# Where the row maxima of an attention kernel get their PSUM tiles: single tiles throughout, or from step 140 on pairs of maxima that share three score tiles with the scores

## The chip, the cores and the metric

The kernel runs on one core of one Trainium2 chip. The metric is the device time of one execution in microseconds (us). The kernel before takes 1129.84 us, the median of three runs from 1128.42 to 1130.21. "Step 140" and the like are numbers of attention steps, counted from 0, and are explained below.

## The reference

In short form: one block of a transformer on 2048 tokens of width 448, in float32: a layer norm with a modulation from the vector `c`, full attention with 16 heads of 28 columns, its output projection, a gate and a residual, then a second modulated layer norm and a channel MLP (448 to 1792 to 448, GELU) with its own gate and residual.

```python
mod = (_silu(c) @ w_mod).reshape(c.shape[0], 6, 1, -1)
sa, ca, ga, sb, cb, gb = (mod[:, i] for i in range(6))
h = _layernorm(x) * (1 + ca) + sa
q, k, v = (h @ wqkv) split into 16 heads of 28
p = softmax(q @ k.T * 28 ** -0.5)
x = x + ga * ((p @ v) @ wo)
h = _layernorm(x) * (1 + cb) + sb
x = x + gb * (gelu(_layernorm(h) @ w1 + b1) @ w2 + b2)
```

## The kernel before

The program has three stretches: a first one that makes queries, keys and values (up to about 169 us of the profile), the attention loop (169 to 833 us) and the MLP. The change is in the attention loop.

**Units and steps.** The 16 heads make four groups `g` of four heads, and the 2048 queries four blocks `qt` of 512. One pair (g, qt) is a unit, 16 units in all, and each unit walks through the 2048 keys in 16 steps (`kt`) of 128 keys. So there are 256 steps; step = 16 u + kt.

**What a step does.** For each half of the four heads (two heads) TensorE computes scores, 128 keys on the partitions by 512 queries for two heads, into one score tile of two PSUM banks (`s0` or `s1`, 128x2x512 floats). A score is the sum of three matmuls per head, since every operand is split into a high and a low float32r part; that makes 6 matmuls per half and 12 per step (line 1162). A matmul of one head uses 28 or 29 of the 32 rows of one of TensorE's four row groups: the first half of the heads lives in row groups 0 and 1, the second in 2 and 3. In the text, S1 is the half that is written first in a step and S2 the other. ScalarE takes the exponential of a whole score tile (line 1167), once per half. Then TensorE multiplies the exponentials of the step before with the values (line 1132, "output products", into tile `o`), with all 128 rows.

**Row maxima.** The softmax subtracts each query's maximum before the exponential. It goes into the score matmul as a 29th row of the queries, so it has to be known before the unit starts. A maximum is computed for 128 queries of one head over 512 keys: one matmul of the high parts alone (line 466, in one row group) into a single PSUM bank, and one reduction on VectorE from there (line 471). A unit needs 64 of these; they stand in a queue `mxq` that is sorted by unit. When a unit's 64 are done, `max_fin` reduces over the key blocks (line 502), and two steps later `put` transposes the result (line 509) and sends it into the unit's query tile with four DMAs. `finish_max` computes what is left of the next unit's maxima, at key step 10 of each unit.

**PSUM.** Eight banks: `o` has one, `s0` and `s1` two each, `m1` one, and `m2` two tiles of one bank each. In the attention loop single maxima take turns in `m1`, `m2`, `m2`. When no maximum is left, `third_tile` gives the two banks of `m2` to a third score tile `s2`.

**What sets the order.** Everything is written out by hand (`manual_schedule`): the engines take their instructions in the order of the Python code, and the framework adds semaphores where a tile is still in use. It tracks a tile as a whole, not its halves. `n_maxima` gives 4 maxima to even steps and 3 to odd ones. They are written between the score matmuls of the step: one or two behind the first terms of S1, in the row groups of S2, and the rest behind the last term of S2.

**Projection.** In the last group, and already for the last block of the group before, the output of a finished unit is multiplied with `wo` in key steps 8 to 11 of the next unit (`t_wo`, one product of 128 tokens per step, "projection steps": 200 to 203, 216 to 219, 232 to 235 and 248 to 251). It takes 9 or 12 matmuls of 448 columns (line 386) into a tile of `m1` or `m2`, and ScalarE copies it out (line 926). Its input goes a long way first: the unit's output is copied to `osb` (line 1101), its denominators go to DRAM and back, are inverted on VectorE (line 886) and broadcast by DMA; GpSimd multiplies (line 895, `t_split`), VectorE rounds (line 905, the high part `hi`, in `t_split2`) and GpSimd subtracts (line 906, the low part). The plan in `unit_end_tasks` puts `t_split2` five steps behind the first task of a unit's end. In steps 228 to 235 the first layer norm of the MLP stretch also starts (lines 190, 191, 207, on VectorE).

## Time and profile before

| what | value |
|---|---|
| median of three runs | 1129.84 us |
| profiled execution | 1130.08 us |
| its span, first to last instruction | 1128.0 us |
| TensorE clock granted | 1.000 |
| attention steps 140 to 235 | 514.85 to 778.13 us |
| maxima in steps 140 to 233 | 323 |

In the profile's rows PE is TensorE's matmul, PEld its weight load, DVE is VectorE, ACT is ScalarE, POOL is GpSimd and SP is SyncE, which issues DMAs. A row reads: start, duration, engine, line, operation, output tile <- input tiles (buffer numbers are left out, so `s` is any score tile and `m` any tile of a single maximum), partitions x elements, count; in brackets the idle time ahead of it and what ended it. In rows of groups the two numbers behind the bar are busy time in us and mean duration in ns.

### The profile page before, as it was taken

The numbers are of one execution on the slowest core, as the hardware profiler recorded it, in microseconds if no ns is written. First come the engines' busy times: TensorE is split into PE (matmuls) and PEld (weight loads), VectorE is DVE, ScalarE is ACT, GpSimd is POOL, SyncE is SP. The second block draws the span as 40 slices with busy tenths as digits, with TensorE's granted clock in tenths as the row PEclk, the third lists the DMA queues.
The fourth block names the chain that finished last, engine by engine and source line by source line (L and its number), as shares of the span: only waits on it lengthen the run. The fifth ranks groups of instructions, "written<-read, shape, count | busy, mean of one in ns | idle before, by whom it ended". The sixth has DMA issues, their size and how long they took to land.

```text
span 1128.0 us, 20665 instructions
## 1 busy us (share of the span) xinstructions
PE 1116.4 (99%) x8319; PEld 670.1 (59%) x8319; DVE 843.7 (75%) x1485; ACT 672.0 (60%) x823; POOL 209.6 (19%) x211
## 2 busy tenths in 40 slices
PE   8999999999999999999999999999999999999998
PEld 6756674444444444444444454545468888888887
DVE  6968788999999999999999978595448853444322
ACT  4555657888887888788788867576752321111110
POOL 1533332110000000000000020217114504123000
PEclk9999999999999999999999999999999999999999
DMA  9562263121121211311111312020422100000000
GB/s 303 202 200 88 91 200 114 48 84 41 58 95 57 58 40 57 91 53 58 53 44 58 112 41 83 4 85 1 137 73 78 35 33 1 1 33 1 33 1 33
DMA packets 49341, 81.19 MB, mean 72 GB/s; under 512 B 12311, under 2 KB 18702, under 8 KB 49234
## 3 DMA queue, kind: packets, MB, share of 16 engines
q1 hardware_dynamic: 48762, 79.14, 22.1%
q8 instruction: 65, 1.06, 0.4%
q10 hardware_dynamic: 148, 0.46, 0.1%
q0 software_dynamic: 336, 0.28, 0.1%
q14 instruction: 30, 0.25, 0.1%
HBM read 55.04 MB, written 26.48 MB: 72 GB/s over the span
## 4 chain that ended last, share of the span: by engine, by line
PE 94%; DVE 3%; ACT 1%; DMA 1%; issue 1%; POOL 0%; SPq 0%; DVEq 0%; ACTq 0%; POOLq 0%
PE s L1162 26%; PE o L1132 22%; PE m L386 16%; PE pa L386 8%; PE m L466 6%; PE s L1232 3%; PE s L1233 3%; PE s L1231 3%; DVE mxp L471 2%; PE t L1232 1%; PE t L1233 1%; PE t L1231 1%; DMA slot_c<-in_w_mod_dram 1%; PE ma L466 1%; PE o L267 1%
## 5 line engine op out<-in xcount | busy, mean ns | idle before, releaser
L471 DVE TENSOR_REDUCE mxp<-m 128x1 f32<-128x512 f32 x884 | 568.8, 686 | 75.3 <-PE m L466 41.1
L1162 PE MATMUL s<-slot_b,slot_a 28*128 28x512 f32 (+1 forms) x3072 | 376.3, 420 | 0.0
L1162 PEld LDWEIGHTS s<-slot_b,slot_a 28*128 28x128 f32 (+1 forms) x3072 | 213.0, 184 | 247.4 <-ACT slot_c L1167 124.1
L466 PE MATMUL m<-kh,qh 28*128 28x512 f32 x863 | 287.6, 472 | 1.2 <-DVE mxp L471 0.9
L1167 ACT ACTIVATE slot_c<-s 128x1024 f32<-128x1024 f32 x170 | 174.3, 1025 | 75.9 <-PE s L1162 75.6
L1132 PE MATMUL o<-slot_c,v 128*32 128x512 f32 x680 | 178.8, 605 | 0.0
L1208 ACT ACTIVATE full<-m,b_col 128x512 f32<-128x512 f32 x56 | 38.6, 689 | 192.0 <-PE m L386 175.5
L1132 PE MATMUL o<-slot_c1h,v 128*32 128x512 f32 x512 | 134.7, 605 | 0.0
L1132 PE MATMUL o<-slot_c0h,v 128*32 128x512 f32 x512 | 134.7, 605 | 0.0
L1167 ACT ACTIVATE slot_c0h<-s 128x1024 f32<-128x1024 f32 x128 | 130.4, 1019 | 2.4 <-PE m L386 2.4
L1167 ACT ACTIVATE slot_c1h<-s 128x1024 f32<-128x1024 f32 x128 | 130.4, 1019 | 0.0
L1211 DVE CAST hi<-full 128x512 fp32r<-128x512 f32 x56 | 25.5, 455 | 134.6 <-ACT full L1208 134.6
L466 PEld LDWEIGHTS m<-kh,qh 28*128 28x128 f32 x863 | 114.3, 182 | 8.6 <-DVE mxp L471 5.1
L1167 ACT ACTIVATE slot_d<-s 128x1024 f32<-128x1024 f32 x86 | 88.1, 1025 | 39.3 <-PE s L1162 39.1
L895 POOL TENSOR_TENSOR osb<-osb,osb 128x512 f32<-128x512 f32 x16 | 20.9, 1307 | 441.1 <-DMA osb<-drec 356.8
L1132 PE MATMUL o<-slot_d,v 128*32 128x512 f32 x344 | 90.5, 605 | 0.4 <-ACT osb L1101 0.4
L386 PE MATMUL m<-y,slot_a 128*128 128x512 f32 x160 | 60.7, 395 | 0.0
L1132 PEld LDWEIGHTS o<-slot_c,v 128*32 128x32 f32 x680 | 24.5, 108 | 52.4 <-issue 49.5
L1212 DVE TENSOR_TENSOR lo<-full,hi 128x512 fp32r<-128x512 f32 x56 | 44.2, 788 | 5.9 <-DVE hi L1211 0.9
L471 DVE TENSOR_REDUCE mxp<-ma 128x1 f32<-128x512 f32 x54 | 35.6, 683 | 7.1 <-PE m L466 4.8
L386 PE MATMUL m<-y,slot_v 128*128 128x512 f32 x112 | 39.2, 396 | 0.0
L386 PE MATMUL m<-y,slot_b 128*128 128x512 f32 x112 | 39.0, 398 | 0.0
(316 smaller groups left out, 1626.7 us busy)
## 6 DMA issues: line engine op xcount, KB each, us to landing
slot_b<-d SPq DMA_DIRECT2D x32, 256.0 KB
slot_a<-d SPq DMA_DIRECT2D x32, 256.0 KB
d<-lo SPq DMA_DIRECT2D x28, 256.0 KB
d<-hi SPq DMA_DIRECT2D x16, 256.0 KB
osb<-drec SPq DMA_DIRECT2D x15, 256.0 KB
out_dram<-xn SPq DMA_DIRECT2D x16, 224.0 KB
raw<-in_B_w_dram SPq DMA_DIRECT2D x14, 224.0 KB
qh<-d SPq DMA_DIRECT2D x12, 256.0 KB
```

The source lines that it names most:

```text
L386: pe.matmul(p, a, b, start=(i == 0), stop=(i == len(terms) - 1))
L466: pe.matmul(m, qh_sb[(g, qt)][js, i * 128 : (i + 1) * 128], k[js, :], start=True, stop=True)
L471: dve.tensor_reduce(out=mxp[(g, qt)][:, i, j, cch : cch + 1], in_=m, op=ALU.max, axis=AX.X)
L1132: pe.matmul(o[32 * j : 32 * j + 32, :], v_sb[kt // 4][:, kt % 4, 4 * g + j, :], p[j // 2][:, j % 2, :], start=(kt == 0), stop=(kt == NKT - 1),
L1162: pe.matmul(s2[:, jj, :], ks[rows_, kp, kc], qs[rows_, qp, :], start=(term == 0), stop=(term == 2))
L1167: act.activation(pt[hf], s2, AF.Exp, scale=SCALE)
L1208: act.activation(gf, p, AF.Gelu_apprx_tanh, bias=b1_col[:, i : i + 1])
L1211: dve.tensor_copy(ghi, gf)
L1212: dve.tensor_tensor(out=glo, in0=gf, in1=f(ghi), op=ALU.subtract)
L1231: pe.matmul(pp, ghi[:, ts], w_hi, start=(m == 0), stop=False)
L1232: pe.matmul(pp, ghi[:, ts], w_lo, start=False, stop=False)
L1233: pe.matmul(pp, glo[:, ts], w_hi, start=False, stop=(m == NFT - 1))
```

## The change

Nothing is changed in the computation. Ahead of step 140 step 0 computes two maxima fewer, and the choice of the next maximum is a little different. From step 140 on (`RING`):

- The tiles of `m2` are given up at step 140, and `s2` exists from there on. S1 always goes into `s0`. `s1` and `s2` take turns: in one step the one holds the scores of S2 and the other a pair of maxima, in the next step the other way round. Which half of the heads is S1 alternates from step to step.
- A step computes three maxima: one single in `m1`, behind the first term of S1, and one pair, two neighbouring heads of the same queries and keys, ahead of the last term of S2 (`emit_pair`). A pair is two matmuls into the two halves of one score tile and one reduction of 128x2x512 on VectorE (line 614). A fourth maximum comes only where `extra` finds that the steps left won't do; it does so once, at step 193.
- In a projection step `t_wo` writes a second pair into `s0` and a single into the second half of the score tile that this step's S2 has used, and then the projection itself into the first half of that same tile. That makes six maxima.
- `finish_max` comes at key step 12 instead of 10, and `ready_max` passes only maxima whose query and key tiles have been loaded three steps ago.

In the built program steps 140 to 235 hold 325 maxima, of them 104 pairs; the last is in step 235 (before: in step 233). In steps 200 to 203, 216 to 219 and 232 to 234 there are six per step, and `finish_max` finds four left ahead of step 220.

The core of the diff:

```diff
+LAST_MAX = NKT - 4
+RING = 140
...
+    def emit_single(half, ps):
+        near = ready_max()
...
+        max_one(g, qt, cch, i, j, ps)
+        count(g, qt, [cch])
+
+    def emit_pair(half, t):
+        near = ready_max()
+        for a, m in enumerate(near):
+            n = m[:4] + (m[4] + 1,)
+            if m[4] == 2 * half and n in near:
+                mxq.remove(m)
+                mxq.remove(n)
+                g, qt, cch, i, j = m
+                for jj in range(2):
+                    max_mm(g, qt, i, j + jj, kh_sb[(g, cch)], lambda: t[:, jj])
+                dve.tensor_reduce(out=mxp[(g, qt)][:, i, j : j + 2, cch], in_=t, op=ALU.max, axis=AX.X)
+                count(g, qt, [cch, cch])
+                return
+        for jj in range(2):
+            emit_single(half, lambda: t[:, jj])
...
         def t_wo(t):
             def go():
-                p = ps_mx()
+                if three:
+                    p = ps_mx()
+                else:
+                    emit_pair(0, ps_two("s0"))
+                    two = ps_two(now[0])
+                    emit_single(1, lambda: two[:, 1])
+                    p = two[:, 0]
...
-            if kt == NKT - 6 and u + 1 < NU:
+            clock[0] = step
+            if kt == LAST_MAX and u + 1 < NU:
                 finish_max(*divmod(u + 1, NB))
...
+            now[0] = turns[step % 2]
+            first = step % 2 if step >= RING else 0
+            if step == RING:
                 third_tile(True)
+            ring = step >= RING
+            more = ring and not three and extra(step)
+            late_one, after = after, more
+            n_max = 0 if ring else 4 - step % 2
...
-            for hf in range(2):
-                s2 = ps_s2()
+            for n, hf in enumerate((first, 1 - first)):
+                s2 = ps_s2() if three else ps_two((now[0] if n else "s0") if ring else ("s0", "s1")[n])
                 for term, (kp, qp) in enumerate(((0, 0), (1, 0), (0, 1))):
+                    if ring and n == 1 and term == 2 and mxq:
+                        emit_pair(first, ps_two(turns[1 - step % 2]))
                     for jj in range(2):
                         rows_ = slice(64 * hf + 32 * jj, 64 * hf + 32 * jj + DH + (term == 0))
                         pe.matmul(s2[:, jj, :], ks[rows_, kp, kc], qs[rows_, qp, :], start=(term == 0), stop=(term == 2))
...
+                    if ring and (n, term) == ((1, 0) if late_one else (0, 0)) and not three:
+                        emit_single(1 - first, ps_mx)
```

Three places of TensorE's order follow, of the program before and of the changed one. Lines 1162, 466, 1132 and 386 (scores, maxima, output products, projection) are lines 1228, 470, 1188 and 390 in the changed kernel. `s0`, `s1`, `s2`, `m1`, `m2` and `o` are the PSUM tiles, with numbers of their uses behind them; `slot_a` and `slot_b` hold keys and queries for the scores, `kh` and `qh` those for the maxima, `slot_c`, `slot_d` the exponentials. In brackets are the engines that a row waits for ("Activation" is ScalarE).

First, TensorE in one plain step of three maxima, step 143 of the program before:

```order
L1162 MATMUL s1_1695_7078<-slot_b0_1442_6028,slot_a3_1567_6552 128x512 [waits Activation_49]
L1162 MATMUL s1_1695_7078<-slot_b0_1442_6028,slot_a3_1567_6552 128x512
L466 MATMUL m1_1696_7081<-kh0_1107_4625,qh3_1226_5113 128x512 [waits DVE_49]
L1162 MATMUL s1_1695_7078<-slot_b0_1442_6028,slot_a3_1567_6552 128x512 x4
L1162 MATMUL s0_1697_7089<-slot_b0_1442_6028,slot_a3_1567_6552 128x512 [waits Activation_49]
L1162 MATMUL s0_1697_7089<-slot_b0_1442_6028,slot_a3_1567_6552 128x512 x5
L466 MATMUL m2_1698_7096<-kh0_1107_4625,qh3_1226_5113 128x512 [waits DVE_49]
L466 MATMUL m2_1699_7099<-kh0_1107_4625,qh3_1226_5113 128x512 [waits DVE_49]
L1132 MATMUL o_1577_6591<-slot_c0_1685_7042,v3_231 32x512 x2
L1132 MATMUL o_1577_6591<-slot_c0h_1686_7043,v3_231 32x512 x2
```

and step 151 of the changed program:

```order
L1228 MATMUL s0_1744_7317<-slot_b1_1574_6581,slot_a1_1499_6268 128x512 [waits Activation_49]
L1228 MATMUL s0_1744_7317<-slot_b1_1574_6581,slot_a1_1499_6268 128x512
L470 MATMUL m1_1745_7320<-kh2_1203_5028,qh3_1250_5224 128x512 [waits DVE_49]
L1228 MATMUL s0_1744_7317<-slot_b1_1574_6581,slot_a1_1499_6268 128x512 x4
L1228 MATMUL s2_1746_7328<-slot_b1_1574_6581,slot_a1_1499_6268 128x512 [waits DVE_49]
L1228 MATMUL s2_1746_7328<-slot_b1_1574_6581,slot_a1_1499_6268 128x512 x3
L470 MATMUL s1_1747_7333<-kh1_1231_5149,qh3_1250_5224 128x512 [waits Activation_49]
L470 MATMUL s1_1747_7333<-kh1_1231_5149,qh3_1250_5224 128x512
L1228 MATMUL s2_1746_7328<-slot_b1_1574_6581,slot_a1_1499_6268 128x512 x2
L1188 MATMUL o_1699_7122<-slot_d0_1736_7286,v1_229 32x512 x2
L1188 MATMUL o_1699_7122<-slot_c0h_1737_7287,v1_229 32x512 x2
```

The two maxima behind S2 have become a pair in a score tile ahead of the last term of S2; S2 waits for VectorE instead of ScalarE, and the pair for ScalarE.

Second, TensorE in projection step 217 from S2 (before) on; the first two products of the projection end the piece:

```order
L1162 MATMUL s0_2327_9735<-slot_b1_2110_8812,slot_a2_2068_8639 128x512 [waits Activation_49]
L1162 MATMUL s0_2327_9735<-slot_b1_2110_8812,slot_a2_2068_8639 128x512 x5
L466 MATMUL m2_2328_9742<-kh0_1717_7166,qh3_1832_7642 128x512 [waits Activation_49]
L1132 MATMUL o_2248_9411<-slot_d0_2313_9672,v2_230 32x512 x2
L1132 MATMUL o_2248_9411<-slot_c0h_2314_9673,v2_230 32x512 x2
L386 MATMUL m1_2329_9750<-slot_e0_489_2037,slot_a2h_2258_9448 128x448 [waits DVE_49]
L386 MATMUL m1_2329_9750<-slot_e1_490_2038,slot_a2h_2258_9448 128x448
```

and in the changed program from the last term of S2 on:

```order
L1228 MATMUL s2_2214_9491<-slot_b1_2028_8623,slot_a2_1994_8469 128x512 x2
L1188 MATMUL o_2149_9199<-slot_d0_2201_9427,v2_230 32x512 x2
L1188 MATMUL o_2149_9199<-slot_c0h_2202_9428,v2_230 32x512 x2
L470 MATMUL s0_2216_9507<-kh3_1833_7720,qh2_1689_7068 128x512 [waits Activation_49]
L470 MATMUL s0_2216_9507<-kh3_1833_7720,qh2_1689_7068 128x512
L470 MATMUL s2_2217_9511<-kh0_1727_7243,qh3_1835_7725 128x512 [waits Activation_49]
L390 MATMUL s2_2217_9511<-slot_e0_489_2037,slot_a2h_2158_9234 128x448 [waits DVE_49]
L390 MATMUL s2_2217_9511<-slot_e1_490_2038,slot_a2h_2158_9234 128x448
```

A pair in `s0` and a single in `s2` stand between the output products and the projection, and the projection's first product, into that same `s2`, waits for VectorE. The count that this wait asks for is reached by the reduction of the single just ahead of it.

Third, TensorE between steps 219 and 220: the last product of the projection, and then, before:

```order
L386 MATMUL m2_2347_9844<-slot_e0_489_2037,lo_2304_9632 128x448
L1162 MATMUL s1_2351_9862<-slot_b1_2110_8812,slot_a3_2099_8772 128x512 [waits Activation_49]
L1162 MATMUL s1_2351_9862<-slot_b1_2110_8812,slot_a3_2099_8772 128x512
L466 MATMUL m1_2352_9865<-kh1_1757_7331,qh3_1832_7642 128x512 [waits DVE_49]
L1162 MATMUL s1_2351_9862<-slot_b1_2110_8812,slot_a3_2099_8772 128x512 x2
```

and in the changed program:

```order
L390 MATMUL s2_2236_9614<-slot_e0_489_2037,lo_2194_9395 128x448
L470 MATMUL m1_2238_9632<-kh2_1799_7578,qh2_1689_7068 128x512
L470 MATMUL m1_2239_9635<-kh2_1799_7578,qh2_1689_7068 128x512 [waits DVE_49]
L470 MATMUL m1_2240_9638<-kh3_1833_7720,qh2_1689_7068 128x512 [waits DVE_49]
L470 MATMUL m1_2241_9641<-kh3_1833_7720,qh2_1689_7068 128x512 [waits DVE_49]
L1228 MATMUL s0_2245_9649<-slot_b1_2028_8623,slot_a3_2019_8588 128x512 [waits PE_49]
L1228 MATMUL s0_2245_9649<-slot_b1_2028_8623,slot_a3_2019_8588 128x512
L470 MATMUL m1_2246_9652<-kh1_1774_7460,qh3_1835_7725 128x512 [waits DVE_49]
L1228 MATMUL s0_2245_9649<-slot_b1_2028_8623,slot_a3_2019_8588 128x512 x4
```

Four singles of `finish_max` stand ahead of step 220, all in `m1`, and three of them wait for VectorE; the step's own single in `m1` is the next to wait.

## The prediction

> **What bounds the kernel now.** I read the page first (busy times, the chain that ended last), then time by stretches of the attention loop, then the timeline of single steps.

> ```profile
> PE 1116.4 (99%) x8319; PEld 670.1 (59%) x8319; DVE 843.7 (75%) x1485; ACT 672.0 (60%) x823; POOL 209.6 (19%) x211
> PE 94%; DVE 3%; ACT 1%; DMA 1%; issue 1%; POOL 0%; SPq 0%; DVEq 0%; ACTq 0%; POOLq 0%
> 514.85:661.66 146.81, 91.01 (x720) 51.57 (x720) 1.00 0.22 69
> 661.66:678.89 17.23, 5.43 (x48) 3.11 (x48) 1.00 0.00 1
> 678.89:708.26 29.37, 17.63 (x144) 10.07 (x144) 1.00 0.26 83
> 708.26:728.69 20.43, 5.81 (x49) 3.19 (x50) 1.00 0.01 2
> 728.69:758.86 30.17, 17.59 (x144) 10.03 (x144) 1.00 0.25 80
> 758.86:778.13 19.27, 5.00 (x49) 2.73 (x50) 1.00 0.01 1
> ```

> The chain is TensorE's: 94% of the span. The other rows are stretches of time with the score matmuls in them, 12 to a step (a 49th reaches over from the next): steps 140 to 199 are 60 steps in 146.81 us, 2.45 each; the third and fifth row are 12 plain steps each, the others 4 projection steps each. All plain steps from 140 to 231 are 84 in 206.4 us, the projection steps 12 in 56.9 us. The timeline of two plain steps shows what fills 2.45 us:

> ```profile
> 522.49 0.49 PE L1162 MATMUL s<-slot_b,slot_a 29*128 29x512 f32 x2
> 522.74 0.74 PE L1162 MATMUL s<-slot_b,slot_a 29*128 29x512 f32 x8
> 523.28 0.40 PE L466 MATMUL m<-kh,qh 28*128 28x512 f32 x2
> 523.32 0.40 PE L1162 MATMUL s<-slot_b,slot_a 28*128 28x512 f32 x2
> 523.49 1.02 ACT L1167 ACTIVATE slot_c<-s 128x1024 f32<-128x1024 f32 x1 [0.80 <-PE s L1162]
> 523.65 0.62 PE L1132 MATMUL o<-slot_c,v 128*32 128x512 f32 x2
> 524.41 1.02 ACT L1167 ACTIVATE slot_c1h<-s 128x1024 f32<-128x1024 f32 x1
> 524.64 0.50 PE L1162 MATMUL s<-slot_b,slot_a 29*128 29x512 f32 x2
> 525.50 0.49 PE L466 MATMUL m<-kh,qh 28*128 28x512 f32 x1
> 526.05 0.40 PE L1162 MATMUL s<-slot_b,slot_a 28*128 28x512 f32 x2
> 526.39 0.62 PE L1132 MATMUL o<-slot_c,v 128*32 128x512 f32 x2
> 527.38 0.50 PE L1162 MATMUL s<-slot_b,slot_a 29*128 29x512 f32 x2
> ```

> A step of three maxima runs from 522.49 to 524.64, 2.15 us, and one of four from 524.64 to 527.38, 2.74 us. In the first, S2 starts at 522.74 and shares its time with S1 (eight score matmuls in 0.74 us). In the second S2 has to wait until the exponential that began at 524.41 has left its only tile at 525.43; what is written behind it moves 0.07 us later (525.50). So the two score tiles cost every other step some 0.6 us. In both steps the first exponential starts 1.00 after the step, the second 0.92 later; from the last score pair to the output products 0.33 pass (523.32 to 523.65, 526.05 to 526.39), from S2's start 0.91 (522.74 to 523.65), and from the output products to the next step 1.00.

> **The change part by part.** *Plain steps.* A step has two loops now; call its time P. The pair goes into the tile that held S2 of the step before, free when that step's second exponential ends, 1.00 + 0.92 + 1.02 = 2.94 after that step's start, plus 0.06 to wake: p = 3.00 - P in its own step. Output products 0.33 later and 1.00 to the next step give P = 4.33 - P, so 2.17. The other loop goes over VectorE:

> ```profile
> 714.35 0.51 PE L466 MATMUL m<-kh,qh 28*128 28x512 f32 x2
> 714.92 1.89 DVE L471 TENSOR_REDUCE mxp<-m 128x1 f32<-128x512 f32 x3 [2.90 <-PE m L466]
> L471 DVE TENSOR_REDUCE mxp<-m 128x1 f32<-128x512 f32 x326 | 209.3, 686 | 35.3 <-PE m L466 25.8 <-PE s L1162 2.3
> L502 DVE TENSOR_REDUCE m<-mxp 128x16 fp32r<-128x64 f32 x6 | 1.3, 220 | 0.2
> L207 DVE TENSOR_SCALAR xn<-acc,mv,rs 128x448 f32<-128x448 f32 x4 | 2.8, 688 | 0.0
> L190 DVE BATCH_NORM_STATS2 st<-acc 128x6 f32<-128x448 f32 x4 | 2.5, 619 | 0.0
> ```

> A reduction starts 0.57 after its matmul, 0.46 where that takes 0.39 and not 0.5; I take 0.50. The trace has none of 1024 elements. From 64 and 512 elements (220 and 686 ns) one more costs 1.04 ns, which makes 1.22 us; two singles, 1.37, are the upper bound. S2 of the next step needs that tile: its start is p + 0.50 + 1.22 + 0.06 - P, and P is that plus 0.91 + 1.00, so 2P = p + 3.69, 3P = 6.69, P = 2.23. This loop binds, since its output products are later than those of the first. With 1.37 it would be 2.28. The 84 plain steps take 187.3 us: **-19.1**. VectorE then has 1.22 + 0.63 (1.89 / 3) of work in 2.23 us, so 0.38 free.

> *Projection steps.* Before:

> ```profile
> 716.49 0.88 PE L386 MATMUL m<-slot_e,slot_a2h 128*128 128x448 f32 x3
> 719.11 0.50 PE L1162 MATMUL s<-slot_b,slot_a 29*128 29x512 f32 x2
> 720.11 1.02 ACT L1167 ACTIVATE slot_c<-s 128x1024 f32<-128x1024 f32 x1 [0.31 <-PE s L1162]
> 720.28 0.62 PE L1132 MATMUL o<-slot_c,v 128*32 128x512 f32 x2
> 721.03 1.02 ACT L1167 ACTIVATE slot_c0h<-s 128x1024 f32<-128x1024 f32 x1
> 721.28 0.47 PE L386 MATMUL m<-slot_e,slot_a2h 128*128 128x448 f32 x1
> ```

> The projection starts 2.17 after its step (719.11 to 721.28), and its 12 products take 2.62 (716.49 to 719.11); with 9, three of about 0.20 fewer, 2.02. In the changed order the second pair stands at 2.17, its tile `s0` being free (first exponential 1.00 + 1.02). The single waits for the second exponential: 720.11 + 0.92 + 1.02 is 2.94 after the step, so 3.00. The first product waits for the reduction of that single, because the semaphores are kept per tile. VectorE takes the pair at 2.17 + 0.50 = 2.67 until 3.89, the single until 4.51 (0.63 more), and the product can start at 4.57: 2.40 later than before, with nothing behind it in TensorE's queue that could fill the time, and with the next scores behind it. The steps: 4 x (4.57 + 2.02) = 26.4, 4 x (4.57 + 2.62) = 28.8, and 3 x 7.19 with step 235, which has no such single and starts at 3.00, 5.62: 27.2. Together 82.3 against 56.9: **+25.4**. The 36 maxima more that these steps take are what pays for three per plain step.

> [...]

> *`finish_max` ahead of step 220.* Four singles in one tile: matmul to reduction 0.57, reduction 0.69, waking 0.06, 1.3 a round and three rounds; the step's own single, in S1, then waits for the fourth and holds the second score term for some 0.7 more: **+4.6**.

> *Guests on VectorE.* In steps 228 to 231 one statistic each (0.62) against 0.38 free: +0.24 each; in 232 to 234 a normalisation of 0.69 ahead of the second pair against 0.18 free (first pair's end 2.49 to 2.67), in 234 a statistic too: +2.15. Together **+3**.

> *The high part of a finished unit's output.* It waits on VectorE for GpSimd, and the maxima are queued behind it:

> ```profile
> 644.98 0.59 ACT L1101 COPY osb<-o 128x512 f32<-128x512 f32 x1
> 658.13 1.28 POOL L895 TENSOR_TENSOR osb<-osb,osb 128x512 f32<-128x512 f32 x1 [25.83 <-DMA osb<-drec]
> 691.56 0.59 ACT L1101 COPY osb<-o 128x512 f32<-128x512 f32 x1
> 706.59 1.29 POOL L895 TENSOR_TENSOR osb<-osb,osb 128x512 f32<-128x512 f32 x1 [25.80 <-DMA osb<-drec]
> 741.34 0.59 ACT L1101 COPY osb<-o 128x512 f32<-128x512 f32 x1
> 755.41 1.28 POOL L895 TENSOR_TENSOR osb<-osb,osb 128x512 f32<-128x512 f32 x1 [24.82 <-DMA osb<-drec]
> ```

> From the copy's end to GpSimd's end 13.8, 15.7 and 14.8 us pass, on DMAs that don't get faster. VectorE reaches the instruction seven steps after the unit's first step starts, 7 x 2.23 + 0.3 = 15.9, and the copy ends about 3.0 into it (a step of 2.23, a gap of 0.2 and the copy's 0.59): 12.9 after the copy. So it stands for 0.9, 2.8 and 1.9 us, 5.6 in all; slack of 0.38 a step takes up some: **+4**. Step 0 saves two reductions (1.2 us), and small VectorE instructions between the pairs cost about as much; I leave both out.

> Sum: -19.1 + 25.4 + 4.6 + 3 + 4 = +17.9. The profiled execution took 1130.08 us (2.1 outside its span), 0.2 over the median, so 1130.1 + 17.9 = **1148**.

> **The rivals.** *Faster: TensorE passes over the projection's wait.* For it: the two maxima at 523.28 start ahead of the last score pair at 523.32, behind which they are written. Against it: in the slow step output products whose operands had long been there stand still behind the waiting S2 until 526.39. If it did pass, the projection steps would be 4 x 4.19 and 8 x 4.79, 55.1, the term -1.8 and the time 1121. It decides from a wait of under 2.40 - 17.9 / 11 = 0.77 us a step on.

> *No change: plain steps at the pace of three free score tiles.* After the last maximum the loop already runs so:

> ```profile
> 778.13 0.98 PE L1162 MATMUL s<-slot_b,slot_a 29*128 29x512 f32 x12
> 786.14 0.52 PE L1162 MATMUL s<-slot_b,slot_a 29*128 29x512 f32 x4
> ```

> Four steps in 8.01 us, 2.00 each: 84 of them are 168, the term -38.4, and the time 1129. Against it: there the third tile waits for no pair.

> *Slower still: the plain steps gain nothing,* the pair's wait and VectorE's guests pushing P back to 2.45: 1167. For it: any delay on VectorE now holds S2, where three `m` tiles were a cushion.

> *Slowest: no sharing.* If S2 could no longer share S1's time, every plain step would take the 2.74 of the slow one: 230.2 us, +23.8, 1191. [...]

> **How the numbers follow.** The forecast's own cases, P from 2.17 to 2.28 and the three smaller terms at half or one and a half times, lie between 1137 and 1159: 0.70. No gain 0.11, no sharing 0.02, the pace of three tiles 0.08 (half of it within 0.2% either way, a quarter each side), passing over 0.07, other gains 0.02. The range goes from 1132, towards the pace of three tiles, to 1162, towards no gain. Faster by over 0.2% (2.3 us, about what this kernel's runs can tell from no change) 0.11, within it 0.04, slower 0.85.

> **What would show it.** Right: plain steps of about 2.2 us with every S2 sharing S1's time; in projection steps TensorE idle for over 2 us ahead of the first product, ended by VectorE's reduction; four single reductions in a row ahead of step 220; reductions of 1024 elements at about 1.2 us; VectorE waiting a few us for GpSimd's multiplication in steps 199, 215 and 231. Wrong: projection products that start within 3.1 us of their step, or plain steps of 2.0 us or of 2.45.

## The result, and the profile after

The changed kernel takes 1165.83 us (median of four runs, 1163.27 to 1166.79) against 1129.88 us before on the same chip: a ratio of 1.032, with a 95% interval of 1.030 to 1.034. The forecast was 1148, with a range of 1132 to 1162. The direction was right; the size was not, and the time lies above the range. The profiled execution took 1163.27 us, 1161.5 of them in the span.

From the page of the kernel after: busy time of each engine, the granted clock in 40 slices, the shares of the chain that ended last, and the group of the pairs' reductions.

```profile
PE 1122.2 (97%) x8319; PEld 669.8 (58%) x8319; DVE 840.7 (72%) x1381; ACT 671.4 (58%) x823; POOL 209.4 (18%) x211
...
PEclk9999999999999999999999998898999999999999
...
PE 89%; DVE 5%; DMA 3%; ACT 1%; issue 1%; POOL 0%; SPq 0%; DVEq 0%; POOLq 0%; ACTq 0%
...
L614 DVE TENSOR_REDUCE mxp<-s 128x2 f32<-128x1024 f32 x104 | 127.4, 1225 | 7.7 <-PE s L470 3.7
```

TensorE still carries the chain, but VectorE now has 5% of it, where it had 3, and the row of the clock has a dip that the kernel before did not have. A reduction of 1024 elements takes 1225 ns; it was put at 1.22 us. The next fence has time by stretches, with the score matmuls in them, as it was shown of the kernel before: steps 140 to 199, projection steps 200 to 203, plain steps, projection steps 216 to 219, plain steps, steps 232 to 235. The third number from the end is the granted clock.

```profile
516.02:651.88 135.86, 79.80 (x721) 48.53 (x722) 1.00 0.25 74
651.88:679.89 28.01, 4.98 (x50) 2.90 (x50) 0.94 0.00 1
679.89:706.71 26.82, 15.71 (x144) 9.46 (x145) 1.00 0.28 90
706.71:746.61 39.90, 6.21 (x48) 3.39 (x48) 0.86 0.00 1
746.61:777.25 30.64, 17.83 (x145) 10.59 (x146) 0.91 0.25 79
777.25:812.09 34.84, 6.79 (x48) 3.60 (x49) 0.90 0.00 1
```

Before, these six took 146.81, 17.23, 29.37, 20.43, 30.17 and 19.27, 263.3 in all; now 296.1, 32.8 more, and these 96 steps hold nearly all of the 33.5 by which the span grew. The 72 plain steps of the first and third row take 162.7 us, 2.26 each (forecast 2.23, before 2.45). The projection steps pay for it. In the second row the clock is at 0.94 and in the last three at 0.86 to 0.91, although not one of these rows stood below 1.00 before.

A plain step up to the start of its successor, TensorE in order of time, and ahead of it the reduction of the pair of the step before:

```profile
522.30 1.23 DVE L614 TENSOR_REDUCE mxp<-s 128x2 f32<-128x1024 f32 x1
...
523.20 0.50 PE L1228 MATMUL s<-slot_b,slot_a 29*128 29x512 f32 x2
...
523.54 0.77 PE L1228 MATMUL s<-slot_b,slot_a 28*128 28x512 f32 x8
523.99 0.40 PE L470 MATMUL s<-kh,qh 28*128 28x512 f32 x2
...
525.46 0.50 PE L1228 MATMUL s<-slot_b,slot_a 29*128 29x512 f32 x2
```

From 523.20 to 525.46 are 2.26 us; eight score matmuls of both tiles share 0.77 us, and the pair's two matmuls (523.99, into a score tile) start within that time. S2 starts 0.34 after its step (523.54), 0.01 behind the end of the reduction that frees its tile (522.30 + 1.23): the wait on VectorE that the forecast had. A projection step (202), with VectorE:

```profile
666.73 0.49 PE L1228 MATMUL s<-slot_b,slot_a 29*128 29x512 f32 x2
...
667.98 1.23 DVE L614 TENSOR_REDUCE mxp<-s 128x2 f32<-128x1024 f32 x1
...
668.86 0.50 PE L470 MATMUL s<-kh,qh 28*128 28x512 f32 x2
669.40 1.23 DVE L614 TENSOR_REDUCE mxp<-s 128x2 f32<-128x1024 f32 x1 [0.20 <-PE s L470]
669.73 0.49 PE L470 MATMUL s<-kh,qh 28*128 28x512 f32 x1 [0.37 <-ACT slot_c0h L1238]
670.55 0.68 DVE L475 TENSOR_REDUCE mxp<-s 128x1 f32<-128x512 f32 x1
671.28 0.88 PE L390 MATMUL s<-slot_e,slot_a2h 128*128 128x448 f32 x3 [1.06 <-DVE mxp L475]
...
673.32 0.50 PE L1228 MATMUL s<-slot_b,slot_a 29*128 29x512 f32 x2
```

The second pair starts 2.13 after the step, the single 3.00, the first product 4.55, and the step takes 6.59: the forecast had 2.17, 3.00, 4.57 and 6.59. Steps 201 to 203 are all like this (6.56, 6.59, 6.57), and steps 218 and 233, with twelve products, take 7.24 and 7.30 (forecast 7.19). So the mechanism of the projection step was read rightly. One sign of it did not show: TensorE stands idle for 1.43 us in the step, in two waits (0.37 and 1.06), and not for over 2 us, since the three matmuls of the maxima lie in that time. But four steps of that kind were forecast at 26.4 and took 28.01, because step 200 took 8.29.

### The profile page after: what moved, and what is told of

Same layout as the page of the kernel before. It is cut to its first block, busy times and chain, and to the rows that moved or that the text cites. A ratio compares the mean times of both kernels' runs of the same rounds, so it can differ in the third digit from the quotient of the medians.

```text
span 1161.5 us, 20564 instructions
## 1 busy us (share of the span) xinstructions
PE 1122.2 (97%) x8319; PEld 669.8 (58%) x8319; DVE 840.7 (72%) x1381; ACT 671.4 (58%) x823; POOL 209.4 (18%) x211
## 3 DMA queue, kind: packets, MB, share of 16 engines
q8 instruction: 65, 1.06, 0.4%
## 4 chain that ended last, share of the span: by engine, by line
PE 89%; DVE 5%; DMA 3%; ACT 1%; issue 1%; POOL 0%; SPq 0%; DVEq 0%; POOLq 0%; ACTq 0%
PE s L1228 24%; PE o L1188 20%; PE m L390 13%; PE pa L390 8%; PE m L470 5%; PE s L390 3%; PE s L1303 3%; PE s L1302 3%; PE s L1304 3%; DVE mxp L475 2%; DVE mxp L614 2%; PE s L470 2%; PE t L1303 1%; PE t L1304 1%; PE t L1302 1%; DMA drec<-den 1%
## 5 line engine op out<-in xcount | busy, mean ns | idle before, releaser
L475 DVE TENSOR_REDUCE mxp<-m 128x1 f32<-128x512 f32 x660 | 429.4, 686 | 105.2 <-PE m L470 69.0
L1228 PE MATMUL s<-slot_b,slot_a 28*128 28x512 f32 (+1 forms) x3072 | 363.9, 424 | 1.7 <-DVE mxp L614 0.8
L1228 PEld LDWEIGHTS s<-slot_b,slot_a 28*128 28x128 f32 (+1 forms) x3072 | 210.0, 185 | 238.5 <-ACT slot_c L1238 125.1
L470 PE MATMUL m<-kh,qh 28*128 28x512 f32 x639 | 229.9, 477 | 5.8 <-DVE mxp L475 5.6
L614 DVE TENSOR_REDUCE mxp<-s 128x2 f32<-128x1024 f32 x104 | 127.4, 1225 | 7.7 <-PE s L470 3.7
L470 PEld LDWEIGHTS m<-kh,qh 28*128 28x128 f32 x639 | 89.6, 183 | 13.1 <-DVE mxp L475 10.5
L470 PE MATMUL s<-kh,qh 28*128 28x512 f32 x224 | 53.7, 452 | 4.4 <-ACT slot_c1h L1238 1.9
```

The source lines that it names most:

```text
L470: pe.matmul(m, qh_sb[(g, qt)][js, i * 128 : (i + 1) * 128], k[js, :], start=True, stop=True)
L475: dve.tensor_reduce(out=mxp[(g, qt)][:, i, j, cch : cch + 1], in_=m, op=ALU.max, axis=AX.X)
L614: dve.tensor_reduce(out=mxp[(g, qt)][:, i, j : j + 2, cch], in_=t, op=ALU.max, axis=AX.X)
L1228: pe.matmul(s2[:, jj, :], ks[rows_, kp, kc], qs[rows_, qp, :], start=(term == 0), stop=(term == 2))
```

## Where the forecast's 15 us are missing

Against the forecast the profiled steps 140 to 235 are 14.9 us longer (296.1 against 263.3 + 17.9). Step by step the excess over the forecast's own terms sits here (the other steps make up the rest):

| place | measured, us | forecast there, us | excess |
|---|---|---|---|
| 72 plain steps, and a fourth maximum in step 193 | 162.7 | 160.6 | 2.1 |
| step 200 | 8.29 | 6.59 | 1.7 |
| step 216 | 13.97 | 7.19 + 2.8 (high part) | 4.0 |
| steps 219 and 220 | 11.14 + 5.43 | 7.19 + 2.23 + 4.6 | 2.6 |
| steps 231 to 235 | 37.3 | 29.4 + 1.9 (high part) + 2.4 (guests) | 3.6 |

The last four places, 11.9 us together, are just those around which the granted clock drops to a half. The trace shows four such times: 656.68 to 660.09, 711.29 to 721.53, 745.43 to 752.25 and 800.04 to 806.87, 27.3 us in all. They begin and end on a grid: each lasts 3.41 us or two or three times that, and their starts lie 16, 10 and 16 times 3.413 us apart. Stretches of that grid, with TensorE's busy time and the clock:

```profile
653.27:656.68 3.41, 1.98 (x12) 1.00 0.00 0
656.68:660.09 3.41, 3.41 (x9) 0.50 0.00 0
...
707.88:711.29 3.41, 1.59 (x13) 1.00 0.00 0
711.29:714.71 3.42, 2.69 (x13) 0.50 0.02 5
```

Here the stretches in which TensorE was busy for 1.98 and for 1.59 of 3.41 us were each followed by one at half clock. What makes TensorE idle are for the most part waits that the forecast had named (step 234 is taken up further below). At 708 it is the high part of the finished unit:

```profile
706.93 1.26 POOL L940 TENSOR_TENSOR osb<-osb,osb 128x512 f32<-128x512 f32 x1 [25.13 <-DMA osb<-drec]
708.22 0.43 DVE L950 CAST hi<-osb 128x512 fp32r<-128x512 f32 x1 [3.46 <-POOL osb L940]
708.57 0.68 DVE L475 TENSOR_REDUCE mxp<-m 128x1 f32<-128x512 f32 x1
...
709.30 0.50 PE L470 MATMUL m<-kh,qh 28*128 28x512 f32 x1 [2.09 <-DVE mxp L475]
```

The other two waits of VectorE for this instruction:

```profile
777.06 0.43 DVE L950 CAST hi<-osb 128x512 fp32r<-128x512 f32 x1 [1.01 <-POOL osb L940]
...
840.62 0.43 DVE L950 CAST hi<-osb 128x512 fp32r<-128x512 f32 x1 [1.17 <-POOL osb L940]
```

VectorE waited 5.6 us for GpSimd there, three times in all. The sum is the forecast's, the places are not: 3.46 us ahead of the maxima of step 216 (forecast 2.8), 1.01 in step 231 (1.9), nothing in step 199 (0.9), and 1.17 in step 248, behind the last maximum. In step 216 that cost TensorE 2.09 us of idleness, up to 709.30, and then 10.24 us at half clock in which the projection of step 216 fell. My theory after this view: **each wait cost what it was put at, and the clock charged for it once more.** The rival: the low clock stands beside the waits and costs nothing, since TensorE waits anyhow, and the waits themselves were put too low.

**The same steps with and without half clock.** Two of the kernels below, e5_finfill and e6_pairs, differ from the kernel after only from the end of step 219 on. Up to there they are the same program, but half clock fell elsewhere. Steps 200 and 202, TensorE's busy time and the clock, in the kernel after and then in e6_pairs:

```profile
651.88:660.17 8.29, 6.86 (x42) 0.79 0.00 0
666.73:673.32 6.59, 5.16 (x37) 1.00 0.00 0
...
650.91:657.64 6.73, 5.31 (x39) 1.00 0.00 0
664.23:672.22 7.99, 6.56 (x36) 0.79 0.00 0
```

Without half clock step 200 takes 6.73 us (6.80 in e5_finfill) instead of 8.29, and step 202, where half clock now stands, 7.99 (7.95) instead of 6.59. So the excess of step 200 is the clock's, at 1.4 to 1.6 us for 3.41 us at half clock, and for this step the rival is out.

## The experiments

All times below are medians, beside the kernel before on the same chip (1128.7 to 1129.4 us). "Less" and "more" are against the 1165.8 us of the kernel after, which was timed with another 1129.9 of the kernel before.

**What a wait of TensorE costs, clock included.** To the kernel before, in steps where nothing of the change is, a wait of known length was added at 12 places; the second kernel has two reductions in place of one.

```
                 s2 = ps_s2()
+                if hf == 0 and step in range(30, 138, 9):
+                    for jj in range(2):
+                        pe.matmul(s2[:, jj, :], ks[:32, 0, kc], qs[:32, 0, :], start=True, stop=True)
+                    for _ in range(1):      # e11_gap2: range(2)
+                        dve.tensor_reduce(out=sbt("scr", [128, 2], bufs=1), in_=s2, op=ALU.max, axis=AX.X)
```

> The kernel before, in which at 12 steps (30, 39 and so on to 129, all ahead of step 140) two more matmuls and one reduction of 1024 elements over their result (1.2 us) stand ahead of the first score tile, so that TensorE stands idle for about 1.5 to 2 us there. It measures what a wait of TensorE costs, clock included. If a wait costs its length alone: some 2 us a place, 24 in all, 1153. If stretches at half clock follow (3.4 us, half of it lost) where the wait makes TensorE's busy share of such a stretch fall under 0.6: up to 1.7 us a place more, 1160 to 1172, and the places without half clock are shorter by that than those with it.

> As the last one, with two such reductions, so that TensorE stands for about 3 us at each of the 12 places. By length alone: 3.2 us a place, 1168. With a stretch of 3.4 us at half clock or two behind nearly every place: 1.7 to 3.4 us a place more, 1185 to 1205.

Measured: 1167.2 us (1164.0 and 1170.5) and 1198.1 us. In the first, TensorE stood idle for 1.31 us at each of the 12 places, always the same length. The next fence has, for the places at step 39 and at step 48, eight steps each, and under them the grid's stretch with the wait and the one behind it.

```profile
265.62:287.20 21.58, 20.26 (x197) 1.00 0.16 51
287.20:310.30 23.10, 21.70 (x197) 0.93 0.21 58
270.28:273.69 3.41, 2.09 (x24) 1.00 0.19 72
273.69:277.10 3.41, 3.41 (x40) 1.00 0.31 74
294.17:297.58 3.41, 2.14 (x24) 1.00 0.35 115
297.58:301.00 3.42, 3.42 (x27) 0.50 0.03 7
```

Four of the 12 places had no half clock behind them: eight steps took 21.58 there, 2.0 over the 19.57 of the kernel before. The other eight had 3.41 us of it, and their eight steps took 23.07 to 23.14. So **3.41 us at half clock cost 1.53 us**, 0.45 of a microsecond for each, on top of a wait that was the same. Which places were hit went with where the wait fell on the grid: at steps 39 and 93 it began just as a stretch began, at steps 30 and 84 it began 0.35 to 0.44 us ahead of the end of one, and nothing followed; where it began 1.7 to 1.85 us into a stretch, or in its last 0.25 us, half clock did. With 2.57 us of idleness 11 of the 12 places had half clock behind them, for 3.4 to 10.2 us, and eight steps took 24.4 to 26.8 where the one place without it (step 57) took 22.86: 0.31 to 0.46 us for each microsecond at half clock.

At 0.45, the 27.3 us in the kernel after come to 12.3 us, an estimate; at 0.31 they would be 8.5. The excess at the four places is 11.9.

**The waits covered with work.** The next four kernels give TensorE matmuls that nobody needs while it waits: the wait stays, and if the theory holds the clock does not fall. The first attempt fills the projection steps alone, a second one place alone, a third all places; a fourth does it with fewer matmuls.

```
                     emit_pair(0, ps_two("s0"))
+                    fill(3)                 # n matmuls of 448 columns into m1
                     two = ps_two(now[0])
                     emit_single(1, lambda: two[:, 1])
+                    fill(6)
                     p = two[:, 0]
```

> The kernel after, plus nine matmuls of 448 columns in each of the 11 projection steps of three tiles: three behind the second pair and six behind the single, into m1, whose results nobody reads. They move nothing that waits; they only give TensorE work while it would stand idle ahead of the first product. Theory A (TensorE's clock is halved after the long idle stretches, and the half-clock stretches of 27.3 us in all cost what the prediction lacked): the granted clock stays at 1.00 through most of the loop and the time falls by 8 to 13 us, to about 1154 to 1158, although work was added. Theory B (the steps 200, 216, 220, 232 and 234 are long for waits that the prediction missized, and the low clock beside them is harmless): the time stays at 1166 or rises by what the added matmuls take, up to 4 us.

Measured: 1168.1 us, so the expectation of the clock theory was missed. In the profile only the drop behind step 200 was gone, which e5_finfill and e6_pairs lack too, without any matmul added there. Step 200 fell from 8.29 to 7.24 us, while its neighbours 201 to 203, which had had the full clock before, rose from 6.57 to 7.02 by the added matmuls. The waits in steps 216, 219 and 234 are elsewhere in the step, and 23.9 us at half clock remained.

```
         while left[(g, qt)] > 0:            # e5_finfill
             emit_max(1)
+            if clock[0] == 220 and left[(g, qt)] > 0:
+                d = ps_two("s0")
+                for _ in range(2):
+                    pe.matmul(d[:, 0, :D], wo_p[0][:, 0, :128], wo_p[0][:, 0, :], start=True, stop=True)
```

> The kernel after, plus two matmuls of 448 columns (results not read) behind each of the first three of the four maxima ahead of step 220, into the score tile s0, which nothing needs at that time. The four maxima still wait for each other's reduction in m1 as before. The clock theory (a stretch of 3.4 us in which TensorE is busy for under 0.6 is followed by one at half clock): TensorE is now busy for over 0.7 of the stretch there, the 6.8 us at half clock from 745 on are gone, and steps 219 and 220 take 3 us less (13.5 instead of 16.6 us); the time is 1162 to 1163. The rival (the reductions alone set these steps): the two steps and the time stay as they were, 1166, or rise by 1.

Measured: 1164.8 us (1160.5 to 1167.6). Missed again: steps 219 and 220 took 17.5 us, not 13.5. The half clock from 745 on was shorter by half, but there was a new stretch of it at 740, ahead of the filled place, and others at 668, 733 and 781; 41 us of the profiled execution ran at half clock, more than in the kernel after. Up to the end of step 219 this is the kernel after, and yet half clock stood at 656.68 there and at 668 here: one filled place proves nothing, and all have to be filled.

Then both edits together (three matmuls instead of two ahead of step 220), and two more:

```
                 s2 = ps_s2() if three else ps_two((now[0] if n else "s0") if ring else ("s0", "s1")[n])
+                if n == 0 and step in (216, 232):      # e9_fillall
+                    for _ in range(8 if step == 216 else 4):
+                        pe.matmul(s2[:, 0, :D], wo_p[0][:, 0, :128], wo_p[0][:, 0, :], start=True, stop=True)
...
         for jj in range(2):
             emit_single(half, lambda: t[:, jj])
+            if jj == 0:
+                d = ps_mx()
+                for _ in range(3):
+                    pe.matmul(d[:, :D], wo_p[0][:, 0, :128], wo_p[0][:, 0, :], start=True, stop=True)
```

> The kernel after with matmuls of 448 columns, whose results nobody reads, at all places where TensorE stood in a wait in the loop from step 200 on: nine in each projection step as in the first run, three behind each of the first three maxima ahead of step 220, eight ahead of the scores of step 216 and four ahead of those of step 232, three between the two singles that stand for a pair in step 234. All waits stay. Clock theory: the granted clock stays at 1.00 to the end of the loop; the first run had 23.9 us at half clock left and took 1168, so 10 to 12 us less, 1155 to 1159, in spite of all added matmuls; steps 216 to 220 then come near the prediction's own terms. Rival (waits alone, the low clock costs nothing since TensorE waits anyway): 1166 to 1172.

Measured: 1163.5 us, in two kinds of runs: 1160.0 and 1161.1 with a clock of 1.000, and 1165.8 and 1166.2 with one of 0.996. The time is above the 1155 to 1159 that were expected, because the added matmuls cost more than I had put down (0.45 us in every projection step, and more in steps 231 and 235). But the same program with nothing else changed took 5.5 us more when an estimated 9.3 us of it (0.004 x 1164 x 2) ran at half clock. The stretches 216 to 219, 220 to 231 and 232 to 235 of the profiled execution:

```profile
707.27:743.28 36.01, 35.44 (x203) 22.37 (x202) 19.01 (x22) 10.00 (x12) 5.91 (x6) 1.00 0.00 1
743.28:772.70 29.42, 28.73 (x281) 12.65 (x282) 23.87 (x32) 23.66 (x25) 1.18 (x1) 1.00 0.27 82
772.70:810.20 37.50, 35.78 (x198) 22.55 (x197) 20.66 (x37) 9.69 (x11) 15.01 (x15) 1.00 0.01 1
```

Steps 216 to 219 take 36.0 instead of 39.9, but the eight matmuls ahead of step 216 lie in step 215, which takes 4.0 instead of 2.2. Steps 215 and 216 together take 13.2 instead of 16.2 (forecast 12.2), steps 219 and 220 14.9 instead of 16.6 (forecast 14.0), with the added matmuls in them, with the waits still there and at full clock. Step 235 takes 9.4 instead of 6.4, however, and with it these 96 steps take 295.7 us against 296.1: the added matmuls cost about what the clock gave.

```
-                    fill(3)
+                    fill(2)                 # e15_light against e9_fillall
...
-                    fill(6)
+                    fill(4)
...
-                for _ in range(3):
+                for _ in range(2):
...
-                    for _ in range(8 if step == 216 else 4):
+                    for _ in range(6 if step == 216 else 2):
...
-            if jj == 0:
-                d = ps_mx()
-                for _ in range(3):
-                    pe.matmul(d[:, :D], wo_p[0][:, 0, :128], wo_p[0][:, 0, :], start=True, stop=True)
```

> As the ninth run with fewer added matmuls, so that hardly any delays what follows: in each projection step two behind the second pair and four behind the single, two behind each of the first three maxima ahead of step 220, six ahead of the scores of step 216 and two ahead of those of step 232; nothing in step 234. Price of half clock by the tenth run: 1.5 us for 3.4 us. With 27 us of it in the kernel after, that makes 12 us at most, less where TensorE waits anyway: 1155 to 1159 here if nearly all of it goes. If the clock matters little: 1163 to 1167.

Measured: 1159.3 us over six runs, which again differ by their clock: 1156.7 at 0.994, 1158 to 1159.5 at 0.992 and 0.993, 1166.0 at 0.987 and 1167.8 at 0.985. From the first to the last that is, by the mean clock, an estimated 21 us more at half clock (0.009 x 1160 x 2) for 11.1 us of time, 0.53 each. So the clock is not incidental: the time of one and the same program follows it.

**The waits taken away.** Four edits move work so that a wait ends. One program's time can differ by 11 us between runs, as above, so where a total changed by 6 us or less (e4_split, e6_pairs, e13_both), the times of the steps say more than the total.

```
                     emit_single(1, lambda: two[:, 1])
-                    p = two[:, 0]
+                    p = ps_mx()             # e2_own: the products go into m1
```

> The kernel after with one edit: the projection's products go into m1 and no longer into the half of the tile whose other half held the single. They no longer wait for the reduction of that single; m1 itself is free when the step's other single has been reduced. The prediction's account (the first product stands at 4.57 us after its step's start because it waits for that reduction): it now starts at about 3.1 us, right behind the matmul of the single, 1.5 us earlier in each of 11 steps, so 16 us less and 1150; with shorter idle stretches the clock has less cause to drop, so up to 10 us less again, 1140. Rival (VectorE's total work in the projection step is the bound, so that what is not waited for ahead of the products is waited for behind them): the steps stay at about 7 us and the time at 1160 or more.

Measured: 1150.0 us, 15.8 less. The total is the one expected; its working is not. In step 201 of this kernel:

```profile
656.80 0.50 PE L1228 MATMUL s<-slot_b,slot_a 29*128 29x512 f32 x2
...
658.26 1.02 ACT L1238 ACTIVATE slot_d<-s 128x1024 f32<-128x1024 f32 x1 [0.83 <-PE s L1228]
...
660.68 0.87 PE L390 MATMUL m<-slot_e,slot_a2h 128*128 128x448 f32 x3
661.29 0.68 DVE L475 TENSOR_REDUCE mxp<-s 128x1 f32<-128x512 f32 x1
```

The product does start ahead of the single's reduction, so that was the wait. But it starts 3.9 us after its step, not 3.1, since the step's own maximum in m1 now waits for the copy of the last projection, and the first exponential comes 1.46 after the step instead of 1.00. Steps 201 to 203 take 5.9 us, 0.66 less and not 1.5. Where half clock had stood in the kernel after, more came off: 2.8 us in step 200 and 3.8 in step 216. 20.5 us at half clock remained, at other places.

```
-                if three:
-                    p = ps_mx()
-                else:
-                    emit_pair(0, ps_two("s0"))
-                    two = ps_two(now[0])
-                    emit_single(1, lambda: two[:, 1])
-                    p = two[:, 0]
+                p = ps_mx()                 # e3_mid
+                mid = None
+                if not three:
+                    def mid():
+                        emit_pair(0, ps_two("s0"))
+                        two = ps_two(now[0])
+                        emit_single(1, lambda: two[:, 1])
...
-                mm_acc(p[:, :D], terms)
+                mm_acc(p[:, :D], terms, mid)   # called halfway through the products
```

> The kernel after with the projection's products begun at once in m1, and the second pair and the single written in the middle of the products instead of ahead of them. Where the wait ahead of the products is what the projection steps pay, their products cover it: such a step takes about 5.2 us instead of 6.6 to 7.5, TensorE is never idle for more than 2 us there, the clock stays at 1.00, and the time comes to 1122 to 1132. Rival (VectorE is the bound of a step with six maxima: two pairs of 1.22 and two singles of 0.69 are 3.8 us, with the copies and additions 6): the steps stay near 6.5 us and the time lies above 1145.

Measured: 1143.2 us, 22.6 less. Steps 200 to 203 take 5.27 to 5.46 (expected 5.2), so VectorE's work is not what sets the 6.6 us of a step with six maxima. The total is above the range because steps 216 (10.8 us) and 219 (10.9) kept the high part's wait and the four leftover maxima, and 10.2 us ran at half clock.

```
-        times = (0, 4, 8, 9) if staged else (0, 1, 4, 5)
+        times = (0, 4, 8, 9) if staged else (0, 1, 4, 6)   # e4_split
```

> The kernel after with the split of a finished unit's output into its high and low part one step later. In the kernel after, VectorE stood 3.5 us in step 215 and 1.0 us in step 231 at the high part, waiting for GpSimd, with the reductions queued behind it, and TensorE waited 2.1 us for them at 709.3. Theory (this wait costs what it was put at, +4, and it also starts the 10 us of half clock behind 711): 4 us less by the wait alone, 8 us less with the clock, so 1158 to 1162. Rival (the projection of step 216 waits anyway, since four steps of six maxima follow): less than 2 us, 1164 to 1166.

Measured: 1159.8 us, 6.0 less: step 216 takes 10.25 instead of 13.97, although a later split costs 2.1 us in step 248, beyond the maxima. As the theory has it, more comes off step 216 than the wait of 2.09.

```
                 finish_max(*divmod(u + 1, NB))     # e6_pairs, ahead of it at step 220:
+                    emit_pair(1, ps_two("s0"))
+                    emit_pair(1, ps_two(turns[step % 2]))
```

> The kernel after with the four maxima left over ahead of step 220 computed as two pairs, one into s0 and one into the tile of the step's second scores, so that no maximum waits for the reduction of the one ahead of it. What the prediction put down for this place (+4.6) and the half clock behind it (3.4) go, and step 220's scores wait for two reductions of 1.2 us instead: about 6 us less, 1159 to 1161. If the place is bound by VectorE's work alone, 4 reductions of 0.69 against 2 of 1.22: less than 1 us, 1165.

Measured: 1162.1 us, 3.7 less, not 6. Steps 219 and 220 take 9.5 + 3.9 instead of 11.1 + 5.4; the pairs' own two reductions still hold step 220, and half clock had moved to other places (34 us in the profiled execution).

**A wait that the forecast had not seen.** In step 234 of the kernel after:

```profile
795.29 0.69 DVE L475 TENSOR_REDUCE mxp<-s 128x1 f32<-128x512 f32 x1
...
796.03 0.50 PE L470 MATMUL s<-kh,qh 28*128 28x512 f32 x1 [0.78 <-DVE mxp L475]
...
798.33 0.68 DVE L475 TENSOR_REDUCE mxp<-s 128x1 f32<-128x512 f32 x1
...
799.06 0.50 PE L470 MATMUL s<-kh,qh 28*128 28x512 f32 x2 [0.88 <-DVE mxp L475]
```

There are no 1024-element reductions here: near the end of the list no two maxima fit each other, and each "pair" is two singles in one tile, the second waiting for the reduction of the first. It is what the forecast had put at 1.3 us a round ahead of step 220, at a place where it had not looked.

```
         for jj in range(2):
-            emit_single(half, lambda: t[:, jj])
+            emit_single(half, lambda: t[:, jj], todo)   # matmul now, reduction into todo
+        for fn in todo:
+            fn()
```

> The kernel after with one edit: where no pair is at hand and two single maxima take its place in one tile, both matmuls now come ahead of both reductions, so that the second no longer waits for the reduction of the first. In step 234 of the kernel after this happened twice (TensorE's waits of 0.78, 0.88 and 1.38 us between 795 and 801). If that is the rest of the error: about 2.5 us less from the waits and up to 3 more where the half clock behind 800 goes too, 1160 to 1163. If VectorE's guests set that step: 1165 to 1167.

Measured: 1162.2 us, 3.6 less; steps 234 and 235 take 15.6 instead of 18.1 us. In the profiled execution 34.1 us ran at half clock, more than the 27.3 of the kernel after, so the 3.6 is not the price of these waits alone. With the filling matmuls of e15_light as well:

> The thirteenth and the fifteenth edit together (the two single maxima with matmuls first, and the added matmuls that keep the clock up). If both shares are what the prediction lacked and the rest of its terms hold, this comes to 1151 to 1154: the 1148 forecast, plus 2 to 4 for the added matmuls and 1 to 2 for the fourth maximum in step 193 and plain steps of 2.25 instead of 2.23. If there is a third cause of some size: above 1156.

Measured: 1156.2 us (1154.1 to 1158.6), 2 over what was expected. The four runs had clocks of 0.992 to 0.997, so an estimated 7 to 18 us at half clock remained (twice what the clock lacks of 1, times the time), and the two with least of it took 1154.1 and 1154.7. The median lies just above the 1156 that was to speak for a third cause. The profiled execution, 1158.6 us, still had 17.1 us at half clock; at 0.45 that is 7.7 us and leaves 1151, an estimate. So no third cause of size is needed, but it is not ruled out either.

**Where else the maxima could go.**

```
-                if three:
-                    p = ps_mx()
-                else:
-                    emit_pair(0, ps_two("s0"))
-                    two = ps_two(now[0])
-                    emit_single(1, lambda: two[:, 1])
-                    p = two[:, 0]
+                p = ps_mx()                 # e8_three
...
-                most = max(most, (need - 3 * n_plain - 6 * n_wo) / n_plain)
+                most = max(most, (need - 3 * n_plain - 3 * n_wo) / n_plain)
```

> The kernel after with projection steps of three maxima, as in the kernel before: no pair and no single ahead of the products, which go into m1; the 32 maxima that they took are spread over plain steps as a fourth one. Price of a fourth maximum in a plain step, from steps 193 to 195 of the kernel after: 2.74 + 2.41 + 2.44 against 3 of 2.24, 0.87 us. Theory (the projection steps and what follows from their waits cost 49 us over what they took before, 102.8 and 3.2 us in step 220 against 56.9): 49 less and 28 more, 1143 to 1148. Rival (a step of four in the new order costs the 2.74 of the old one and projection steps wait for m1 all the same): above 1155.

Measured: 1149.6 us, 16.3 less, a little above what was expected, with 3.4 us at half clock in the profiled execution. In steps 140 to 199 there are 25 maxima more, and these steps take 153.3 instead of 135.9 us: 0.70 for each. So neither place holds them for nothing. The kernel before seems to have had them for nothing: by its rows ahead of the prediction, 0.91 us pass from the start of S2 to the output products in a step of three maxima and in one of four, so that the fourth lies beside the wait for the score tile. In that kernel every slow step has four maxima and every fast one three, so only one step of the record parts the two: step 140 of the kernel after, whose S2 still waits for the exponential of step 139, has three maxima and takes 2.74 us all the same. It is a reading of rows, not an experiment.

**All waits taken away.** e7_best joins e3_mid, the split (two steps later) and the pairs of e6_pairs; e12_unit has in place of the pairs a pick that takes the unit due first; e16_best adds the edit of e13_both and splits the unit that ends ahead of step 224 only one step later.

```
-        times = (0, 4, 8, 9) if staged else (0, 1, 4, 5)
+        times = (0, 4, 8, 9) if staged else (0, 1, 4, 7 if u in (12, 13) else 5)    # e7_best, e12_unit
+        times = (0, 4, 8, 9) if staged else (0, 1, 4, {12: 7, 13: 6}.get(u, 5))     # e16_best
...
-                        emit_pair(0, ps_two("s0"))
+                        emit_pair(None, ps_two("s0"))               # e12_unit, e16_best
...
-                        emit_single(1, lambda: two[:, 1])
+                        emit_single(None, lambda: two[:, 1])
...
+        if half is None:                                            # in emit_single, and so in emit_pair
+            fits = [m for m in near if m[:2] == near[0][:2]]
```

> The projection's products begun at once with the maxima in their middle, as in the third run, and the two other waits taken away as well: the high part of a finished unit's output split two steps later (for the units that end ahead of steps 208 and 224), and the four maxima ahead of step 220 as two pairs. In the third run step 216 was still 4.6 us longer than its neighbours, 219 and 220 together 8 us longer than a projection step and a plain one, and 10.2 us passed at half clock. By the theory (waits that TensorE stands in, plus half clock behind them) all this goes: 10 to 13 us less than 1143, so 1130 to 1133, and the granted clock is 1.00 until the end. If it comes below 1126, the arrangement beats the kernel before. If the rest is VectorE's work, which stays the same: 1138 to 1143.

> As the seventh run (products begun at once, high part split two steps later), but with the two pairs ahead of step 220 taken out again; instead the pair and the single of the projection steps are always taken from the unit that is due first, so that none of its maxima are left over at step 220. Theory (TensorE's waits and the half clock behind them are what is left over the kernel before): steps 219 to 221 come to 6.1, 2.3 and 2.3 us in place of 7.9, 4.6 and 3.6, so 5 us less, 1130 to 1132, about the kernel before. Rival (VectorE's work is the bound and what isn't waited for there is waited for in the steps up to 235): 1134 to 1137.

> The twelfth run (1136) with the edit of the thirteenth, and the split of the unit that ends ahead of step 224 one step later instead of two: in the twelfth run TensorE stood 1.7 us in step 232 for the low part, which came too late, and half clock followed for 6.8 us. Theory: 1.7 + 3 us less there and 1 to 2 in steps 202 and 233 to 235, so 1129 to 1132, level with the kernel before. Rival (VectorE's work in the last projection steps, guests included, is the bound): 1134 to 1137.

Measured: 1135.7, 1136.1 and 1129.0 us. The first fell between its two expectations: 13.7 us at half clock were left, behind the pairs of step 220 and behind the low part of the split, which then came too late for step 232. Against the profiled execution of the first (1137.3 us), the second gained 3.7 us in steps 219 to 221 and lost 1.8 in steps 200 to 203 (1.3 in step 202). Its median is no better because two of the first one's four runs, with less half clock (0.998), took 1134.1. TensorE again stood 1.66 us for the low part in step 232, with 6.8 us at half clock behind it: the time is the rival's. With the low part early again and the singles' matmuls first, the third is level with the kernel before: ratio 0.9996, interval 0.9987 to 1.0005, clock 1.00 until the end. Its six stretches (all instructions):

```profile
516.08:651.91 135.83, 135.83 (x1385) 58.72 (x1381) 117.62 (x136) 117.92 (x125) 10.42 (x12) 1.00 0.25 74
651.91:674.19 22.28, 21.70 (x144) 11.42 (x140) 14.80 (x19) 10.16 (x12) 3.49 (x4) 1.00 0.00 1
674.19:701.69 27.50, 27.25 (x277) 11.53 (x276) 23.28 (x27) 23.40 (x26) 1.48 (x2) 1.00 0.28 88
701.69:726.51 24.82, 24.18 (x156) 13.71 (x153) 15.10 (x20) 10.15 (x12) 5.72 (x6) 1.00 0.01 2
726.51:754.40 27.89, 27.73 (x276) 11.94 (x277) 24.68 (x33) 23.71 (x26) 2.43 (x2) 1.00 0.28 87
754.40:779.32 24.92, 24.29 (x156) 13.84 (x153) 19.22 (x29) 9.85 (x12) 14.66 (x13) 1.00 0.00 1
```

Their sum is 263.24 us, that of the kernel before 263.28. The plain steps give 15.1 us (191.2 against 206.4) and the projection steps take 15.1 (72.0 against 56.9). That is the balance of the new tiles in an order that never cost the clock: nil. No version here beats the kernel before.

## Why the forecast was wrong, by its own steps

- *Plain steps* (-19.1): right in mechanism and nearly in size. 2.25 us against 2.23, and one fourth maximum of 0.9 us in step 193 left out, together 2.1 us. The loop over VectorE binds as described (S2 starts as the pair's reduction ends, 523.53 and 523.54).
- *Projection steps* (+25.4): right. 6.56 to 6.59 and 7.24 to 7.30 against 6.59 and 7.19, wherever the clock was full. (The trace has 72 maxima in the 12 steps against 29 before, 43 more and not 36; the sum does not use this number.) e2_own confirms the wait on the single's reduction; the rival in which TensorE passes over it did not happen: in step 202 the first product started 4.55 us after its step.
- *`finish_max` ahead of step 220* (+4.6): steps 219 and 220 exceed 7.19 and 2.23 by 7.15. The waits are as described, three of 0.78 us ahead of step 220 and one in it; 2.55 us more than forecast, with 6.8 us at half clock beside them.
- *Guests on VectorE* (+3): the normalisations stood where they were expected, but the step missed the four singles in step 234. This is the second thing that the sum lacked; without it steps 234 and 235 take 2.4 us less.
- *The high part* (+4): near in size, and partly by luck. VectorE's waits were 3.46 and 1.01 us, 4.5 in the steps with maxima, but against 2.8, 1.9 and 0.9 forecast each is off by 0.7 to 0.9 us; that all three of the trace again make 5.6 is chance, since one of them lies in step 248. What the wait ahead of step 216 set off was missed.
- **The step that failed** is the sum itself, where it prices the waits: "2.40 later than before, with nothing behind it in TensorE's queue that could fill the time". The forecast saw that TensorE would stand idle in 11 steps and charged the length of the idleness alone. In these traces a stretch of 3.41 us in which TensorE was busy for under 0.60 was followed by half clock 37 of 39 times, at 0.45 us for each microsecond of it by e10_gap1. In the kernel after this makes an estimated 12 of the 14.9 us missing in the profiled execution (17.8 by the medians, of runs with a lower clock, 0.984 to 0.985 against 0.988). No row of the kernel before could have shown it, since its clock stood at 1.00 throughout; but the forecast should have asked what its idle stretches would do, and no rival had it. Since the price depended on where the waits fell on the grid (half clock behind 8 of 12 equal waits in e10_gap1), the honest remedy would have been an upper end of the range some 10 us higher.

What stays open: the exact share of the clock. It is 11.9 us by the excess at the four places, where the singles of step 234 are included, and 12.3 by the price from e10_gap1; by the differences between runs of one program (0.53 and 0.59 for each microsecond) it would be 14 to 16, and by the lowest price of e11_gap2 8.5. Nor do the parts add up: 12 for the clock, 2.4 for step 234 and 2.1 for the plain steps are more than 14.9, so other terms, such as the wait in step 199 that never came, were put too high. For step 200 the clock is shown by the same program with and without it; for steps 216, 220 and 234 it rests on that price and on e9_fillall.

## What to carry to other kernels

A wait of the matmul engine should be priced twice: its length, and half clock behind it. Here half clock followed 37 of the 39 stretches of 3.41 us that were busy for under 0.60, at 0.45 us for each microsecond of it in e10_gap1 and 0.31 to 0.46 in e11_gap2. Work that fits beside a wait was not free where there was no wait: a fourth maximum cost, by the reading above, nothing in a step paced by its score tiles, and 0.70 us in a faster one (e8_three). When work is added to a step whose engine must wait for its result, put it in the middle of work that does not depend on it (in e3_mid 5.45 us against 6.57 in steps 201 to 203, with the same six maxima).
